# Norm gains turned by TensorE, idle products ahead of the first scores, another order of the first loads, and the second half of w_in rounded over eight pairs

## The chip, the cores and the metric

One core of a Trainium2 chip. The metric is the device time of one execution in microseconds (us), lower is better. PE is TensorE (its weight loads are PEld), DVE is VectorE, ACT is ScalarE, POOL is GpSimd, SP is the engine that issues most transfers (SPq is its queue). L405 is line 405 of the kernel in question; the changed kernel's lines stand some 6 to 8 lower in the file, so the scores are L405 before and L413 after.

## The reference

```python
# q, k, v: (8, 12, 448, 64); g_q, g_k: (64,); w_in: (768, 2048); w_out: (2048, 768)
def rmsnorm(x, g):
    return x / np.sqrt(np.mean(x * x, axis=-1, keepdims=True) + 1e-06) * g
q_n, k_n = rmsnorm(q, g_q), rmsnorm(k, g_k)
scores = q_n @ k_n.transpose(0, 1, 3, 2) / sqrt(64)
attn = softmax(scores)                      # over the last axis
x = (attn @ v).transpose(0, 2, 1, 3).reshape(3584, 768)
h = x @ w_in
out = (h / (1 + exp(-h))) @ w_out
```

Both weights arrive as 64-bit floats. The kernel builds 32-bit floats from the two words of each ("rounding").

## The kernel before

48 pairs of heads are run one after the other: six pairs make a batch. TensorE is kept full by a filler: products with w_in of batches that are already done run between the scores and the weighted sums of the pair at hand (from pair 12 on; a little from pair 7 on). Each of them is done by Strassen's scheme, seven products of blocks in place of eight, so sums of blocks of w_in and x are needed, and VectorE evicts and adds.

First, the head: loads, gains, normalisation of the first pair.

```python
    load(state, 0)                       # q, k and v of pair 0, on SP's queue
    for i, g in enumerate((g_q, g_k)):   # both gains as rows, for a check of their size
        nc.scalar.dma_start(g1[:, i, :], g.rearrange("(one d) -> one d", one=1))
    load(state, 1)
    room = Room(nc, const, w_in, z)
    while room.w_in.load():              # the first eight pieces of w_in, 512 KB each
        pass
    for t, g in ((gq2, g_q), (gk2, g_k)):        # both gains as columns, twice
        for half in range(2):
            nc.gpsimd.dma_start(t[ds(half * D, D), :], g.rearrange("(d one) -> d one", one=1))
    # ... (cut)
    nc.gpsimd.tensor_tensor(out=gains, in0=gq2, in1=gk2, op=ALU.mult)
    nc.gpsimd.tensor_scalar(out=gains, in0=gains, scalar1=float(D) ** -0.5, ...)   # cut
```

Second, the ring for w_in. A piece is loaded as raw words into a slot, `open` copies its two words on ScalarE, `round` puts them together on VectorE (L106, L109, L113) and GpSimd (L117), and then loads into every slot that is free:

```python
    def round(self):
        # ... (cut: three instructions on VectorE)
            nc.gpsimd.tensor_tensor(out=wi, in0=wi, in1=low, op=ALU.add)
        while self.load():
            pass
    # ... (cut)
    def weights_in(n, point):            # called at points 0 to 3 of pair n
        if n < 2 * NPAIR:                # pairs 0 to 11: one piece per pair
            count = point == 3
        else:                            # pairs 13 to 16: three pieces per pair
            count = 2 * NPAIR < n < 2 * NPAIR + 5 and point > 0
        for _ in range(count):
            room.w_in.round()
            room.w_in.open()
        i = n - 2 * NPAIR
        if i == 0 and point > 1:
            for step in range(2):
                sum_w_in(1, 2 * (point - 2) + step)
        if i in (1, 5, 6):
            sum_w_in({1: 0, 5: 2, 6: 3}[i], point)
```

In every second pair the softmax sums of two pairs are exchanged between partitions: four small copies, then two that wait for them. Behind them, in the same queue, come the pieces of w_in and then q and k of the pair three ahead.

```python
    for n in range(last + 2):
        load(n + 3, "qk")
        # ... scores, weights_in(n, 0), filler, weights_in(n, 1) (cut)
        divide_by_sums(n)     # n even: sums, reciprocals, then the exchange on SP's queue
        # ... (cut)
        weights_in(n, 3)      # n < 12: round a piece, load the next
        normalise(n + 3)      # ScalarE squares q and k of pair n + 3
```

Of the kernel before, what the change touches and what calls it, by code (L numbers as in the profile page):

```python
# [11 lines left out]
F32 = mybir.dt.float32  # L12
AF = mybir.ActivationFunctionType
ALU = mybir.AluOpType
AX = mybir.AxisListType
# [12 lines left out]
BANK = 512  # L28
# [19 lines left out]
class Rounder:  # L48
# [39 lines left out]
    def round(self):  # L88






        i = self.rounded
        if i == len(self.pieces):
            return
        while self.opened <= i:
            self.open()
        self.rounded += 1  # L100
        dst, src, (_, raw), low = self.pieces[i]
        if src.dtype == I64:
            nc = self.nc
            wi = dst.bitcast(I32)
            high = raw.rearrange("p (n two) -> p n two", two=2)[:, :, 1]
            nc.vector.tensor_scalar(  # L106
                out=dst, in0=dst, scalar1=HIGH_MIN, scalar2=HIGH_MAX, op0=ALU.max, op1=ALU.min
            )
            nc.vector.tensor_scalar(  # L109
                out=wi, in0=wi, scalar1=3, scalar2=0x3FFFFFF8,  # L110
                op0=ALU.logical_shift_left, op1=ALU.bitwise_and,
            )
            nc.vector.scalar_tensor_tensor(  # L113
                out=wi, in0=high, scalar=-(1 << 30), in1=wi,
                op0=ALU.bitwise_and, op1=ALU.bitwise_or,
            )
            nc.gpsimd.tensor_tensor(out=wi, in0=wi, in1=low, op=ALU.add)  # L117
        while self.load():
            pass


class Room:
# [6 lines left out]
    def __init__(self, nc, pool, w_in, z):  # L129
        P = z.P  # L130
        self.NC = z.NF // self.CHUNK
        self.size1 = z.NW * self.COLS
        self.size2 = 3 * z.NW // 2 * self.COLS // 2
        self.all = pool.tile([P, self.NC * (self.size1 + self.size2)], F32, name="W")
        self.rest = self.all[:, ds(self.NC * self.size1, self.NC * self.size2)]


        n = 2 * self.COLS
        bits = self.rest.bitcast(I32)
        pieces, before = [], {}  # L140
        for i in range(self.NC):
            for c in range(z.NW):
                number = len(pieces)
                late = i >= self.NC // 2
                raw = number % (3 if late else 8)
                low = n * (3 if late else 8) + number % 2 * self.COLS
                start = self.NC // 2 * self.size2 if late else 0
                pieces.append(
                    (
                        self.chunk(i)[:, ts(c, self.COLS)],  # L150
                        w_in[ts(c, P), ts(i, self.COLS)],
                        (
                            before.get((late, raw), 7 if late else None),
                            bits[:, ds(start + raw * n, n)],
                        ),
                        bits[:, ds(start + low, self.COLS)],
                    )
                )
                before[late, raw] = number
        self.w_in = Rounder(nc, pieces)  # L160
# [13 lines left out]
def kernel(  # L174
# [22 lines left out]
    nc = tc.nc  # L197
    z = Shapes(q, w_in)
    P, D, R, J = z.P, z.D, z.R, z.J

    const = ctx.enter_context(tc.tile_pool(name="const", bufs=1))

    n = 2 * J * D
# [5 lines left out]
    state = [dict() for _ in pairs]  # L209
# [3 lines left out]
    def load(state, n, names="qkv"):  # L213
        if n >= len(pairs):
            return
        b, hp = pairs[n]
        for name in names:

            order = "p j h d" if name == "k" else "p h j d"
            t = rings[name][n % len(rings[name])]  # L220
            t = t.rearrange(f"p ({order[2:]}) -> {order}", h=2, j=J)
            nc.sync.dma_start(
                t, sources[name][b, ts(hp, 2)].rearrange(f"h (p j) d -> {order}", j=J)
            )
            state[n][name] = t if name != "k" else t.rearrange("p j h d -> p h j d")


    load(state, 0)
    g1 = const.tile([1, 2, D], F32, name="g1")
    gq2 = const.tile([P, 1], F32, name="gq2")  # L230
    gk2 = const.tile([P, 1], F32, name="gk2")
    gains = const.tile([P, 1], F32, name="gains")
    for i, g in enumerate((g_q, g_k)):
        nc.scalar.dma_start(g1[:, i, :], g.rearrange("(one d) -> one d", one=1))
    load(state, 1)
    room = Room(nc, const, w_in, z)
    while room.w_in.load():
        pass
    minus_half = const.tile([P, 1], F32, name="minus_half")
    nc.gpsimd.memset(minus_half, -0.5)  # L240
    for t, g in ((gq2, g_q), (gk2, g_k)):
        for half in range(2):
            nc.gpsimd.dma_start(t[ds(half * D, D), :], g.rearrange("(d one) -> d one", one=1))
    ident = const.tile([P, P], F32, name="ident")
    make_identity(nc, ident)
    ones = const.tile([P, D], F32, name="ones")
# [3 lines left out]

    small = const.tile([1, 1], I32, name="small")
    most = const.tile([1, 1], F32, name="most")
    both = const.tile([1, D], F32, name="both")
    nc.vector.tensor_tensor(out=both, in0=g1[:, 0, :], in1=g1[:, 1, :], op=ALU.mult)
    nc.vector.tensor_reduce(
        out=most, in_=both, axis=AX.X, op=ALU.max, apply_absolute_value=True
    )
    nc.vector.tensor_scalar(
        out=small, in0=most, scalar1=float(SCORE_MAX / D**0.5), scalar2=None, op0=ALU.is_le
    )  # L260

    nc.gpsimd.tensor_tensor(out=gains, in0=gq2, in1=gk2, op=ALU.mult)
    nc.gpsimd.tensor_scalar(
        out=gains, in0=gains, scalar1=float(D) ** -0.5, scalar2=None, op0=ALU.mult
    )


    normal = [const.tile([R, J, 2, D], F32, name=f"qn{i}") for i in range(2)]
# [44 lines left out]
            engine.tensor_tensor(out=by_head, in0=rows["q"], in1=factor, op=ALU.mult)  # L313


def store(nc, out, z, column, o, m0):


    at = 0
    while at < o.shape[0]:  # L320
        b, c = divmod(column + at, z.S)
        j, p = divmod(c, z.R)
        n = min(z.R - p, o.shape[0] - at)
        rows = out[ds(b * z.S, z.S), ds(m0, o.shape[1])].rearrange("(p j) m -> j p m", j=z.J)
        nc.sync.dma_start(rows[j, ds(p, n)], o[ds(at, n), :])
        at += n


# [1 line left out]
def bounded(  # L330
# [41 lines left out]
    def normalise(n):  # L372
        if n <= last:
            normalise_rows(
                nc, z, state[n], normal[n % 2], squares, rms[n % 4], minus_half, nc.gpsimd
            )

    def transpose(n, name):
# [349 lines left out]
    def halves_out(t):  # L728
        w = tiles[t % 2].rearrange("p (m r t c) -> p m r t c", m=HF, r=2, t=2)
        s = s_tiles[t % 2].rearrange("p (s m c) -> p s m c", s=3, m=HF)  # L730
        a11, a12, a21, a22 = (w[:, :, i, j] for j in range(2) for i in range(2))
        left_sums(a11, a12, a21, a22, s[:, 0], s[:, 1], s[:, 2])
        lefts = {"1": a11, "2": a12, "3": s[:, 2], "4": a22, "5": s[:, 0], "6": s[:, 1], "7": a21}

        def right(name, m):
            b11, b12, b21, b22, t1, t2, t4 = chunk_out(m // 2)
            return {"1": b11, "2": b21, "3": b22, "4": t4, "5": t1, "6": t2, "7": b12}[name][
                :, m % 2
            ]

        o = [outs[(2 * t + i) % len(outs)] for i in range(2)]
        done = {(i + 1, j + 1): o[i][:, ts(j, z.HALF)] for i in range(2) for j in range(2)}
        steps = [2 * i + k for i in ORDER for k in range(2)]
        part = Seven(lambda name, m: lefts[name][:, m], right, steps, z.HALF, done)
        yield from chain(part.two(), part.five())
        for i in range(2):
            if t < NT // 2 - 1 or i == 0:
                store(nc, out, z, (2 * t + i) * P, o[i], 0)
            else:
                for j in (1, 0):  # L750
                    store(nc, out, z, (2 * t + i) * P, o[i][:, ts(j, z.HALF)], j * z.HALF)


    filler = dict(work=iter(()), due=0.0, share=0.0)
# [36 lines left out]
    products = HF * 7 * HW * S  # L791
    NPAIR = z.NPAIR

    def weights_in(n, point):

        if n < 2 * NPAIR:
            count = point == 3
        else:
            count = 2 * NPAIR < n < 2 * NPAIR + 5 and point > 0
        for _ in range(count):  # L800
            room.w_in.round()
            room.w_in.open()
        i = n - 2 * NPAIR
        if i == 0 and point > 1:
            for step in range(2):
                sum_w_in(1, 2 * (point - 2) + step)
        if i in (1, 5, 6):
            sum_w_in({1: 0, 5: 2, 6: 3}[i], point)

    transpose(0, "k")  # L810
    normalise(1)
    transpose(0, "q")
    load(2, "qk")
    for n in range(last + 2):
# [5 lines left out]
        if n > 0:  # L820
# [3 lines left out]
            unload(n - 1)  # L824
            if ends and n <= last:
                sum_x([b - 2, b - 1], 1)
        transpose(n + 1, "q")
        if n == 0:
            normalise(2)
        weights_in(n, 0)  # L830
        if ends and n <= last:
# [11 lines left out]
        divide_by_sums(n)  # L843
        if n <= last:
            scores(n, 1)
        if b == 0:
            transpose(n + 1, "k")
        if n <= last:
            weigh(n, 0)
        if b > 0:  # L850
            transpose(n + 1, "k")
        if n <= last:
# [246 lines left out]
```

## Time and profile before

| | |
|---|---|
| median | 1464.22 us (1463.85 to 1465.36, 4 runs) |
| span of the profiled run | 1461.4 us |
| TensorE without a product | 36.4 us of it |
| first scores start | 14.59 us |
| scores of pair 1 start | 26.50 us |

A page of the profile gives busy time per engine. The view by windows gives it per stretch. The timeline gives instructions in order, with the idle time of the engine before each and the event that ended it in brackets. The lines are shown in the prediction below. They are read thus: TensorE is busy 98% of the span, so a change is worth what it takes from the few stretches where TensorE has nothing to do (the first 15 us, some 15 us up to 300 us) or runs slowly.

One more table serves below: the start of the first exponential of each pair, taken from the trace, because it tells where one kernel gets ahead of another. For the kernel before: pair 1 at 29.60, pair 6 at 73.59, pair 13 at 156.64, pair 21 at 311.94 us.

### The profile page before, as it was taken

To read this page: it belongs to the slowest core of one execution; us is meant where nothing else is said; L and a number is where in the kernel's file an instruction comes from. 1 tells how busy PE (TensorE), PEld (TensorE's weight loads), DVE (VectorE), ACT (ScalarE), POOL (GpSimd) and SP (SyncE) were. 2 spreads that over 40 slices of the span, in tenths; PEclk is the share of its full clock that TensorE was granted. 3 is DMA by queue.
4 is the path that set the end of the run, shared out by engine and by line. 5 is a ranking of instruction groups with operands and counts; after the bars stand their busy time and mean duration, and the time that the engine had idled before them with its cause. 6 is when DMAs were issued, how large, how long until landed. Compare 5 with 4: busy or idle time off the path is not lost.

```text
span 1461.4 us, 13997 instructions
## 1 busy us (share of the span) xinstructions
PE 1425.0 (98%) x5024; PEld 693.9 (47%) x5024; DVE 708.7 (48%) x939; ACT 540.5 (37%) x907; POOL 402.6 (28%) x258
## 2 busy tenths in 40 slices
PE   5999999999999999999999999999999999999998
PEld 2333333444444444444444445555555555555554
DVE  4988877646644455745545687722222222222220
ACT  5876566555555455555445344300000000000000
POOL 6665454333333333332322054410000000000000
PEclk9999999999999999999999999999999999999999
DMA  6543253322232232223221157422222222222220
GB/s 211 139 127 103 71 177 97 111 73 60 76 98 70 63 94 77 70 66 97 68 60 70 61 180 241 126 94 80 79 82 82 81 80 83 80 87 83 86 62 25
DMA packets 124180, 137.67 MB, mean 94 GB/s; under 512 B 50500, under 2 KB 104772, under 8 KB 124100
## 3 DMA queue, kind: packets, MB, share of 16 engines
q1 hardware_dynamic: 123968, 136.67, 31.0%
q8 instruction: 42, 0.69, 0.2%
q14 instruction: 38, 0.31, 0.1%
q0 software_dynamic: 128, 0.00, 0.0%
q10 hardware_dynamic: 4, 0.00, 0.0%
HBM read 88.48 MB, written 41.29 MB: 89 GB/s over the span
## 4 chain that ended last, share of the span: by engine, by line
PE 85%; DVE 4%; issue 1%; DMA 1%; ACT 0%; POOL 0%; SPq 0%; DVEq 0%; ACTq 0%; POOLq 0%
PE mm L531 38%; PE sc L531 14%; PE sc L405 8%; PE av L421 8%; PE av L531 7%; PE tr L531 7%; PE tr L449 1%; PE tr L391 1%; PE tr L386 1%; DVE work L433 1%; DVE rms L303 1%; DMA rows<-in_v_dram 0%; DVE work L453 0%; DVE stage L482 0%; DVE W L482 0%
## 5 line engine op out<-in xcount | busy, mean ns | idle before, releaser
L410 ACT ACTIVATE work<-sc,rms 112x448 f32<-112x448 f32 x384 | 212.4, 638 | 185.6 <-PE sc L405 158.1
L531 PE MATMUL mm<-x,W 128*128 128x448 f32 x648 | 261.1, 542 | 3.5 <-DVE parts L482 3.2
L309 POOL TENSOR_TENSOR rms<-rms,minus_half 112x16 f32<-112x16 f32 (+1 forms) x49 | 176.3, 3598 | 265.0 <-DVE rms L305 264.4
L531 PE MATMUL mm<-sums_x,W 128*128 128x448 f32 x480 | 195.2, 542 | 3.2 <-DVE parts L482 1.6
L405 PE MATMUL sc<-work 64*112 64x448 f32 x768 | 172.5, 568 | 1.7 <-ACT work L395 0.8
L531 PEld LDWEIGHTS mm<-x,W 128*128 128x128 f32 x648 | 118.5, 190 | 110.2 <-issue 98.9
L421 PE MATMUL av<-work,rows 112*64 112x448 f32 x768 | 165.5, 552 | 0.0
L433 DVE TENSOR_TENSOR work<-work 112x896 f32<-112x896 f32 x144 | 158.0, 1098 | 1.8
L551 POOL TENSOR_TENSOR parts<-parts,stage 128x448 f32<-128x448 f32 (+1 forms) x37 | 41.8, 1129 | 327.5 <-DVE parts L482 323.1
L531 PEld LDWEIGHTS mm<-sums_x,W 128*128 128x128 f32 x480 | 87.7, 190 | 83.3 <-issue 70.6
L405 PEld LDWEIGHTS sc<-work 64*112 64x112 f32 x768 | 61.7, 174 | 103.7 <-issue 77.5
L421 PEld LDWEIGHTS av<-work,rows 112*64 112x64 f32 x768 | 46.6, 136 | 105.4 <-issue 98.0
L551 POOL TENSOR_TENSOR parts<-parts,W 128x384 f32<-128x384 f32 x9 | 9.0, 996 | 307.8 <-DVE parts L482 307.8
L453 DVE RECIPROCAL work<-tr 128x448 f32<-128x448 f32 x25 | 73.9, 2957 | 39.8 <-PE tr L449 39.7
L482 DVE TENSOR_TENSOR stage<-mm,parts 128x448 f32<-128x448 f32 (+1 forms) x59 | 36.2, 616 | 83.5 <-PE mm L531 51.9
L538 ACT COPY stage<-mm 128x448 f32<-128x448 f32 (+1 forms) x34 | 17.9, 526 | 156.4 <-PE mm L531 146.7
L662 ACT ACTIVATE stage<-stage 128x896 f32<-128x896 f32 x64 | 58.5, 945 | 36.6 <-DVE stage L482 35.7
L531 PE MATMUL mm<-W,work 128*128 128x384 f32 x204 | 68.6, 486 | 0.0
L531 PE MATMUL sc<-W,work 128*128 128x384 f32 x192 | 64.5, 486 | 0.0
L397 DVE TENSOR_SCALAR work<-tr,gains 128x448 f32<-128x448 f32 x36 | 24.6, 684 | 75.4 <-PE tr L391 75.4
L303 DVE TENSOR_REDUCE rms<-qn 112x8 f32<-112x512 f32 x49 | 33.4, 682 | 53.4 <-ACT qn L302 53.3
L313 POOL TENSOR_TENSOR qn<-rows,rms 112x512 f32<-112x512 f32 x47 | 56.6, 1205 | 3.7
(157 smaller groups left out, 1784.6 us busy)
## 6 DMA issues: line engine op xcount, KB each, us to landing
hidden<-stage SPq DMA_DIRECT2D x64, 448.0 KB, 2.9
work<-hidden SPq DMA_DIRECT2D x7, 2048.0 KB, 9.6
x<-hidden SPq DMA_DIRECT2D x7, 2048.0 KB, 8.8
W<-in_moe_w_in_dram SPq DMA_DIRECT2D x24, 512.0 KB, 5.2
rows<-in_moe_w_out_dram SPq DMA_DIRECT2D x32, 384.0 KB, 3.2
rows<-in_q_dram SPq DMA_DIRECT2D x48, 224.0 KB, 3.6
rows<-in_k_dram SPq DMA_DIRECT2D x48, 224.0 KB, 4.2
rows<-in_v_dram SPq DMA_DIRECT2D x48, 224.0 KB, 2.7
```

The costliest lines, as they stand in the source:

```text
L303: nc.vector.tensor_reduce(out=rms[:, i], in_=t, axis=AX.X, op=ALU.add)
L309: nc.gpsimd.tensor_tensor(out=flat, in0=flat, in1=half, op=ALU.pow)
L313: engine.tensor_tensor(out=by_head, in0=rows["q"], in1=factor, op=ALU.mult)
L405: nc.tensor.matmul(banks[:, h, 0:S], kT[rows, ts(j, R)], qT[n % 2][rows, :], start=True, stop=True,)
L410: nc.scalar.activation(e[j][:, h, :], banks[:, h, 0:S], AF.Exp, scale=rms[n % 4][:, 1, h, j : j + 1])
L421: nc.tensor.matmul(st["av"][ds(h * D, D), :], st["v"][:, h, j, :], e[j][:, h, :], start=(j == 0), stop=(j == J - 1),)
L433: nc.vector.tensor_tensor(out=t, in0=e[0] if j == 1 else t, in1=e[j], op=ALU.add)
L453: nc.vector.reciprocal(out=r[0], in_=t)
L482: nc.vector.tensor_tensor(out=out, in0=a, in1=b, op=ALU.add)
L531: nc.tensor.matmul(t, self.left(name, s), self.right(name, s), start=s == ends[0], stop=s == ends[1])
L551: nc.gpsimd.tensor_tensor(out=u2, in0=u2, in1=p5, op=ALU.add)
L662: nc.scalar.activation(t, t, AF.Silu)
```

## The change

Its intent: start the scores earlier, at TensorE's full clock, and take VectorE's load in pairs 13 to 16 apart.

```diff
@@ Rounder.round
-        while self.load():
-            pass
+        for _ in range(2):
+            self.load()
@@ Room: nine early slots, two late ones; the low words stay in the slot
-                raw = number % (3 if late else 8)
-                low = n * (3 if late else 8) + number % 2 * self.COLS
-                start = self.NC // 2 * self.size2 if late else 0
+                raw = number % (2 if late else 9)
+                start = (self.NC - 1) * self.size2 if late else 0
+                words = bits[:, ds(start + raw * n, n)]
 ...
-                        bits[:, ds(start + low, self.COLS)],
+                        words.rearrange("p (n two) -> p n two", two=2)[:, :, 0],
@@ the head
-    load(state, 0)
+    load(state, 0, "qk")
+    load(state, 1, "qk")
 ...
-    load(state, 1)
     room = Room(nc, const, w_in, z)
-    while room.w_in.load():
-        pass
+    for n in range(2):
+        room.w_in.load()
+        load(state, n, "v")
 ...
-    for t, g in ((gq2, g_q), (gk2, g_k)):
-        for half in range(2):
-            nc.gpsimd.dma_start(t[ds(half * D, D), :], g.rearrange("(d one) -> d one", one=1))
 ...
-    nc.gpsimd.tensor_tensor(out=gains, in0=gq2, in1=gk2, op=ALU.mult)
+        keep_busy(4)          # idle products of the identity with itself
+        nc.tensor.transpose(column, both.rearrange("p two d -> p (two d)"), ident[0:1, 0:1])
+        nc.vector.tensor_scalar_mul(out=gains, in0=column, scalar1=float(D) ** -0.5)
+        keep_busy(12)
@@ the dates of rounding and sums, i = n - 12
+    rounds = {(1, 1), (1, 3), (3, 1), (3, 3), (4, 1), (4, 3), (5, 3)}
+    rounds |= {(6, 1), (6, 3), (7, 1), (7, 3), (8, 0)}
+    sums_at = {(0, 2): (1, (0, 1)), (0, 3): (1, (2, 3))}
+    for chunk, at in ((0, (2, 0)), (2, (5, 0)), (3, (8, 1))):
+        for step in range(4):
+            sums_at[at[0] + (at[1] + step) // 4, (at[1] + step) % 4] = chunk, (step,)
@@ the order of the first pairs
-    transpose(0, "k")
     normalise(1)
+    transpose(0, "k")
     transpose(0, "q")
 ... pair 0: the transposes of pair 1 come behind all scores and the first weighted sums of pair 0;
 ... pair 1's q is normalised by VectorE, not GpSimd; the last stores alternate between two queues
```

More of the change, by code (lines that the diff above doesn't have):

```diff
@@ L152, in __init__ @@
                         (
-                            before.get((late, raw), 7 if late else None),
-                            bits[:, ds(start + raw * n, n)],
+                            before.get((late, raw), 8 if late else None),
+                            words,
                         ),
-                        bits[:, ds(start + low, self.COLS)],
+                        words.rearrange("p (n two) -> p n two", two=2)[:, :, 0],
                     )
@@ L225, in load @@
             state[n][name] = t if name != "k" else t.rearrange("p j h d -> p h j d")
-    load(state, 0)
+    load(state, 0, "qk")
+    load(state, 1, "qk")
     g1 = const.tile([1, 2, D], F32, name="g1")
-    gq2 = const.tile([P, 1], F32, name="gq2")
-    gk2 = const.tile([P, 1], F32, name="gk2")
     gains = const.tile([P, 1], F32, name="gains")
@@ L252 @@
     most = const.tile([1, 1], F32, name="most")
-    both = const.tile([1, D], F32, name="both")
-    nc.vector.tensor_tensor(out=both, in0=g1[:, 0, :], in1=g1[:, 1, :], op=ALU.mult)
+    both = const.tile([1, 2, D], F32, name="both")
+    wide = [g1[:, i : i + 1, :].to_broadcast([1, 2, D]) for i in range(2)]
+    nc.vector.tensor_tensor(out=both, in0=wide[0], in1=wide[1], op=ALU.mult)
     nc.vector.tensor_reduce(
-        out=most, in_=both, axis=AX.X, op=ALU.max, apply_absolute_value=True
+        out=most, in_=both[:, 0, :], axis=AX.X, op=ALU.max, apply_absolute_value=True
     )
@@ L260, with keep_busy @@
     )
-    nc.gpsimd.tensor_tensor(out=gains, in0=gq2, in1=gk2, op=ALU.mult)
-    nc.gpsimd.tensor_scalar(
-        out=gains, in0=gains, scalar1=float(D) ** -0.5, scalar2=None, op0=ALU.mult
-    )
+    with tc.tile_pool(name="ps_first", bufs=1, space=bass.MemoryType.PSUM) as ps_first:
+        idle = ps_first.tile([P, P], F32, name="idle")
+        column = ps_first.tile([P, BANK], F32, name="column")[:, 0:1]
+        def keep_busy(n):
+            for _ in range(n):
+                nc.tensor.matmul(idle, ident, ident, start=True, stop=True)
+        keep_busy(4)
+        nc.tensor.transpose(column, both.rearrange("p two d -> p (two d)"), ident[0:1, 0:1])
+        nc.vector.tensor_scalar_mul(out=gains, in0=column, scalar1=float(D) ** -0.5)
+        keep_busy(12)
     normal = [const.tile([R, J, 2, D], F32, name=f"qn{i}") for i in range(2)]
@@ L313, in normalise_rows, with store @@
             engine.tensor_tensor(out=by_head, in0=rows["q"], in1=factor, op=ALU.mult)
-def store(nc, out, z, column, o, m0):
-    at = 0
+def store(nc, out, z, column, o, m0, *queues):
+    at, queues = 0, queues or [nc.sync]
     while at < o.shape[0]:
@@ L324, in store @@
         rows = out[ds(b * z.S, z.S), ds(m0, o.shape[1])].rearrange("(p j) m -> j p m", j=z.J)
-        nc.sync.dma_start(rows[j, ds(p, n)], o[ds(at, n), :])
+        queues[0].dma_start(rows[j, ds(p, n)], o[ds(at, n), :])
+        queues = queues[1:] + queues[:1]
         at += n
@@ L374, in normalise @@
             normalise_rows(
-                nc, z, state[n], normal[n % 2], squares, rms[n % 4], minus_half, nc.gpsimd
+                nc, z, state[n], normal[n % 2], squares, rms[n % 4], minus_half,
+                nc.gpsimd if n > 1 else nc.vector,
             )
@@ L750, in halves_out @@
                 for j in (1, 0):
-                    store(nc, out, z, (2 * t + i) * P, o[i][:, ts(j, z.HALF)], j * z.HALF)
+                    store(
+                        nc, out, z, (2 * t + i) * P, o[i][:, ts(j, z.HALF)], j * z.HALF,
+                        nc.scalar, nc.sync,
+                    )
     filler = dict(work=iter(()), due=0.0, share=0.0)
@@ L792, in bounded @@
     NPAIR = z.NPAIR
-    def weights_in(n, point):
-        if n < 2 * NPAIR:
-            count = point == 3
-        else:
-            count = 2 * NPAIR < n < 2 * NPAIR + 5 and point > 0
-        for _ in range(count):
+    rounds = {(1, 1), (1, 3), (3, 1), (3, 3), (4, 1), (4, 3), (5, 3)}
[4 more added lines that the diff above has]
+            sums_at[at[0] + (at[1] + step) // 4, (at[1] + step) % 4] = chunk, (step,)
+    def weights_in(n, point):
+        i = n - 2 * NPAIR
+        if (i < 0 and point == 3) or (i, point) in rounds:
             room.w_in.round()
             room.w_in.open()
-        i = n - 2 * NPAIR
-        if i == 0 and point > 1:
-            for step in range(2):
-                sum_w_in(1, 2 * (point - 2) + step)
-        if i in (1, 5, 6):
-            sum_w_in({1: 0, 5: 2, 6: 3}[i], point)
+        chunk, steps = sums_at.get((i, point), (0, ()))
+        for step in steps:
+            sum_w_in(chunk, step)
+    normalise(1)
     transpose(0, "k")
-    normalise(1)
     transpose(0, "q")
@@ L826, in bounded @@
                 sum_x([b - 2, b - 1], 1)
-        transpose(n + 1, "q")
-        if n == 0:
+        if n > 0:
+            transpose(n + 1, "q")
+        else:
             normalise(2)
@@ L845, in bounded @@
             scores(n, 1)
-        if b == 0:
+        if b == 0 and n > 0:
             transpose(n + 1, "k")
@@ L849, in bounded @@
             weigh(n, 0)
+        if n == 0:
+            transpose(n + 1, "q")
+            transpose(n + 1, "k")
         if b > 0:
```

## The prediction

> **What bounds the kernel now.** I read the page's first section first, then busy time per window, then the timeline of the first 30 us, then the windows again cut at each pair of heads, then the waits.
>
> The page (busy us, share of the span, instructions):
>
> ```profile
> PE 1425.0 (98%) x5024; PEld 693.9 (47%) x5024; DVE 708.7 (48%) x939; ACT 540.5 (37%) x907; POOL 402.6 (28%) x258
> ```
>
> TensorE is the bound: 1425.0 of 1461.4 us, so only 36.4 us of the span are without a product. Whatever this change does, it must find its time in those 36.4 us, or in products that run slower than they could. The windows say where they lie (columns: window, length, then busy us and instruction count of PE, PEld, DVE, ACT, POOL, then clock, DMA share, GB/s):
>
> ```profile
> 0.00:6.30 6.30, 0.00 (x0) 0.02 (x1) 1.31 (x5) 2.22 (x4) 3.24 (x12) 1.00 0.47 127
> 6.30:14.60 8.30, 2.00 (x10) 1.31 (x10) 2.63 (x5) 2.73 (x5) 3.64 (x4) 1.00 1.01 334
> 14.60:20.20 5.60, 4.26 (x13) 1.73 (x13) 0.37 (x2) 2.32 (x4) 3.97 (x2) 1.00 1.04 384
> ...
> 300.00:400.00 100.00, 99.92 (x386) 42.61 (x385) 59.89 (x75) 52.10 (x85) 31.46 (x17) 1.00 0.26 74
> ...
> 850.00:1400.00 550.00, 548.76 (x1659) 314.85 (x1658) 174.15 (x249) 57.74 (x107) 70.47 (x67) 1.00 0.33 103
> ...
> 1450.00:1462.00 12.00, 5.35 (x17) 2.85 (x15) 1.11 (x2) 0.00 (x0) 0.00 (x0) 0.82 0.25 72
> ```
>
> From 300 us to the last store TensorE never waits. The idle time is 12.6 us ahead of the first scores (6.3 + 8.30 - 2.00), about 1.9 us from there to 30 us, some 15 us between 30 and 300 us (of which 9.2 in the stretch that the change rearranges, below), and 6.1 us after the last product. DMA is at 1.0 from 6.3 to 20.2 us.
>
> The timeline of the head (start, duration, engine, line, operation; in brackets the idle time before and its releaser):
>
> ```profile
> 8.54 0.19 POOL L262 TENSOR_TENSOR gains<-gq,gk 128x1 f32<-128x1 f32 x1 [4.31 <-DMA gk<-in_g_k_dram]
> 8.68 3.27 POOL L309 TENSOR_TENSOR rms<-rms,minus_half 112x8 f32<-112x8 f32 x2
> 11.95 0.23 POOL L263 TENSOR_SCALAR gains<-gains 128x1 f32<-128x1 f32 x1
> 12.27 0.64 ACT L395 ACTIVATE work<-tr,gains 128x448 f32<-128x448 f32 x1 [5.44 <-POOL gains L263]
> 14.59 3.33 PE L405 MATMUL sc<-work 64*112 64x448 f32 x8 [0.62 <-ACT work L387]
> ...
> 22.04 0.63 ACT L302 ACTIVATE qn<-rows 112x512 f32<-112x512 f32 x1 [1.21 <-DMA rows<-in_q_dram]
> ...
> 26.50 1.76 PE L405 MATMUL sc<-work 64*112 64x448 f32 x8 [0.46 <-ACT work L395]
> ```
>
> The first scores (14.59) wait for a chain that begins with a tiny load: gains on GpSimd waits for g_k until 8.54, the powers of the norms queue behind it, the second gains instruction behind those, and ScalarE's copy of k behind that. Eight score records took 3.33 us at 14.59 and 1.76 us at 26.50: the first run at half speed.
>
> **What the Trainium skill says.**
> 1. "TensorE: Matmul & The Clock Gate", Part 1 (the HAM clock gate): the array starts at half rate and is released after one fully busy window of about 3.4 us. The trace agrees: records of this shape take 536 ns at best and 1086 at worst. The clock column reads 1.00 in both stretches, so it must be read from durations.
> 2. "DMA: Bandwidth & Descriptors", Specifications: first byte about 1 us on GpSimd's path, about 0.6 us on the sync and scalar path. The trace is harsher: the 0.2 KB loads from GpSimd's queue took 3.7 to 4.9 us to land; the same vectors as rows from ScalarE's queue, issued until 1.48, were used at 3.06.
> 3. "GPSIMD Engine Reference", Key points: GpSimd shares its SBUF interfaces with VectorE and they contend. The trace agrees: VectorE's first rounding step (L106) takes 0.42 us alone and 1.24 us at 193.91, beside GpSimd.
> 4. Same page, "Performance pitfalls for Q7 kernels": a read costs more when its byte step exceeds 8. Low words in place are read with a step of exactly 8, so by the page without penalty; no run shows it yet (L117 takes 1274 ns on packed words).
>
> **The change part by part.**
>
> *a. Gains by TensorE, fewer early bytes, another start order: the head.* Removed: four DMA issues on GpSimd (2.3 us of its sequencer, 1.28 to 3.6) and the wait to 8.54. Then, step by step, with durations of the same instructions:
> - The row sums of q are scaled by 4.92 in the old trace. The power of q can start there: half of 3.27, so 1.63 us, to 6.6. k lands at 6.2 as before (its load is still the second), squares, sum and scale to 7.75, VectorE's q product (0.69) to 8.4, power of k to 9.4.
> - 4 + 12 idle products. A 128-row product of 448 columns takes 4.53/6 = 0.755 us warm (12 records in the merged rows, less the overhang), so 128 columns 0.216 us warm and 0.43 cold. They start near 1.7 us (identity without the DMA issues before it). Cold throughout they end near 8.6; if released halfway, near 7.7. The gains column is turned near 3.5 us; gains is ready by 8.7 on VectorE, in its turn.
> - The branch, k's transposes (0.6 warm) near 8.5 to 9.2. ScalarE now squares both of pair 1's inputs first: k of pair 1 landed at 9.6, with v of pair 0 no longer ahead (224 KB) about 8.3; squared to 9.0. Copy of k to about 9.8, q's transposes, copy of q: first scores at about 11.0 instead of 14.6, saving 3.6 us.
> - Warm scores and transposes: 1.57 us for each of two score groups. In the order after, all scores of pair 0 stand before pair 1's transposes, so no GpSimd product (18.16 to 19.2) stands between. Exponentials of the first half 11.9 to 14.3 (4 x 0.58), squares of pair 2 1.3 us, second half to 17.9, copy of q 0.6, transposes of k 0.6, copy of k 0.65: scores of pair 1 at about 19.8 instead of 26.50. Saving at this point: **6.7 us**, which contains the 3.6 and the warm clock.
> From there the order is that of before and ScalarE (10.00 of 10 us busy from 30 to 40) sets the pace, so the saving is only shifted, not enlarged.
>
> *b. Second half of w_in over eight pairs: the middle.* Windows cut at the first scores of pairs 13, 14, 15, 16, 17, 18:
>
> ```profile
> 155.53:176.20 20.67, 18.86 (x70) 7.94 (x70) 16.66 (x24) 9.49 (x18) 10.00 (x6) 1.00 0.20 62
> 176.20:195.43 19.23, 18.71 (x76) 7.79 (x75) 17.30 (x24) 14.33 (x23) 11.38 (x7) 1.00 0.53 161
> 195.43:216.52 21.09, 18.36 (x68) 7.47 (x67) 16.87 (x24) 12.25 (x21) 11.24 (x7) 1.00 0.60 180
> 216.52:236.40 19.88, 18.78 (x75) 7.80 (x74) 16.16 (x21) 14.56 (x23) 10.74 (x7) 1.00 0.44 122
> 236.40:255.35 18.95, 18.11 (x68) 7.55 (x67) 12.44 (x17) 10.64 (x17) 8.16 (x5) 1.00 0.26 80
> 255.35:274.57 19.22, 18.72 (x76) 7.79 (x75) 13.18 (x15) 10.27 (x18) 5.91 (x4) 1.00 0.34 102
> ```
>
> TensorE loses 1.8, 0.5, 2.7, 1.1, 0.8, 0.5 = 7.5 us here (pair 12 ahead loses 1.7 more, which the change doesn't touch), waiting for evictions on VectorE. VectorE's w_in work isn't reduced, it is moved: a rounding is 0.42 + 0.43 + 0.69 = 1.54 us, a sum step 0.95 us. Before: three roundings in each of pairs 13 to 16, with four sums in 13 also, four sums in 17 and 18. After: two roundings in 13, 15, 16, 18, 19, four sums in 14, four sums and a rounding in 17, a rounding and three sums in 20. Pairs with three roundings alone lost (0.5 + 2.7 + 1.1)/3 = 1.45; I take 0.5 for two. Pairs with four sums lost 0.67. So after: 5 x 0.5 + 3 x 0.67 + 0.3 = 4.8. Saving **2.7 us**.
>
> *c. Last stores on two queues.* The last four issues span 4.89 us on one queue, most of it waiting for VectorE's last sum (1455.54 + 0.56). One issue of about 0.5 us comes off the end: **0.3 us**.
>
> *d. Low words in place*: nothing, if point 4 holds.
>
> Sum: 6.7 + 2.7 + 0.3 = 9.7 us; 1464.06 - 9.7 = **1454.4 us**.
>
> **The rivals.**
> - *The new wait takes the old one's place.* ScalarE must square k of pair 1 before the first copy, and TensorE must finish 16 idle products before the first transpose. If k lands at 9.6 as before and the products stay cold, scores start near 12.2, and with a cold relapse in the gap between pair 0 and pair 1 the head gives 3 us. For: ScalarE is in order; against: eight 512 KB loads no longer queue at 5.27. Total then 1459.
> - *VectorE's load decides the middle, not its bunching.* The work is the same, and pairs 19 and 20, which lose nothing today, get a share. For: pairs 17 and 18 lose though they round nothing. Then b gives 0: 1457. The other way, short bursts vanish behind 18 us of products per pair: b gives 7: 1450.
> - *The early weights become late.* Two pieces instead of eight are loaded up front, so a rounding or an input load behind two 512 KB pieces could wait. For: inputs are used about one pair (9 us) after their issue; against: 3.6 to 5.2 us to landing, and DMA share 0.3 to 0.6 there. It would cost up to 3 us.
>
> **Range and chances.** Head 3 to 9, middle 0 to 6, stores 0 to 0.6: not all ends at once, so 1449 to 1459. Two per cent is 29.3 us; the whole idle time of 36.4 us, less the 6.2 until k lands and some 5 after the last sum, is 25, plus about 4.5 of cold clock. Faster by over 2% is all but impossible: 0.01. Slower by 2% would need a stall of 29 us in a static order with loads far from full: 0.01. Same: 0.98.
>
> **What would show it.** In the changed trace: gains on VectorE before 9 us and no wait of GpSimd for g_k; the first scores near 11 us with eight records in 1.76 us; pair 1's scores near 20 us; every later start earlier by 6 to 7 us until pair 12; VectorE near 14 us per pair in 13 to 20 and TensorE's idle time there near 5 us; rounding on GpSimd still near 1274 ns. Wrong would be: scores past 12 us behind ScalarE's squares or idle products, score records still at 1086 ns, a wait for rows of q or k after 25 us, or the idle time of pairs 13 to 20 at 7 us again.

## The result

The changed kernel takes 1458.38 us (median of 4 runs, 1456.55 to 1459.26) against 1464.22 us. The ratio is 0.9957 (95% interval 0.9940 to 0.9974). A ratio is the mean time of one kernel's fast runs over that of the other's fast runs of the same rounds, so not quite the ratio of the medians quoted. The profiled run is the slowest of the four, 1459.26 us, with a span of 1457.2 us; that of the kernel before took 1463.25 us, so the two profiles lie 4.0 us apart and the medians 5.8.

The page of the changed kernel, busy time:

```profile
PE 1429.4 (98%) x5057; PEld 699.0 (48%) x5057; DVE 708.3 (49%) x941; ACT 540.4 (37%) x907; POOL 397.9 (27%) x251
```

27.8 us are left without a product, but 5.9 us of the products (2.08 + 3.81) are idle ones that compute nothing.

The windows of the changed kernel (columns as in the prediction):

```profile
6.30:14.60 8.30, 5.86 (x37) 3.18 (x35) 3.68 (x9) 5.09 (x11) 5.46 (x3) 1.00 0.89 240
...
20.20:24.30 4.10, 4.10 (x17) 1.16 (x13) 3.83 (x7) 4.10 (x9) 2.39 (x3) 0.68 0.44 118
...
50.00:75.00 25.00, 21.49 (x94) 7.51 (x94) 19.87 (x26) 19.56 (x37) 14.65 (x7) 0.86 0.63 171
```

The head is fuller, as meant. New is the last line: 3.5 us idle between 50 and 75 us, where the kernel before lost 1.0, and the clock column falls to 0.86.

The timeline of the changed kernel's head:

```profile
5.19 1.65 POOL L315 TENSOR_TENSOR rms<-rms,minus_half 112x8 f32<-112x8 f32 x1 [3.81 <-DVE rms L311]
...
7.75 0.15 DVE L270 TENSOR_SCALAR gains<-column 128x1 f32<-128x1 f32 x1
...
8.80 0.63 ACT L403 ACTIVATE work<-tr,gains 128x448 f32<-128x448 f32 x1 [0.46 <-PE tr L399]
...
10.72 1.76 PE L413 MATMUL sc<-work 64*112 64x448 f32 x8 [0.62 <-ACT work L395]
...
19.30 3.29 PE L413 MATMUL sc<-work 64*112 64x448 f32 x8 [0.79 <-ACT work L403]
```

GpSimd's powers start at 5.19 instead of 8.68 us, the gains are there at 7.9, k is copied at 8.80 instead of 12.27, and the first scores run at full clock from 10.72 us. Pair 1's scores start at 19.30 instead of 26.50 us. But they take 3.29 us: the clock has fallen back.

The first exponential of each pair, in the changed kernel less that of before (from the two traces; negative is earlier):

```
pair    1      3      4      5      6      9     12     13     14     16     17     19     20     21     47
     -7.20  -6.69  -4.63  -2.60  -1.88  -2.10  -1.80  -1.80  -3.87  -9.51  -7.03  -6.78  -5.75  -4.08  -4.09
```

This difference is called the shift below, and this row is the whole account of these two profiles. The head brings 7.2 us. **4.8 us are lost between pairs 3 and 6.** The middle brings 7.7 us up to pair 16 and gives 5.4 of them back by pair 21, 2.3 net. From pair 21 on the two kernels run at the same pace to a hundredth.

The stall, in the changed kernel's timeline of 42 to 63 us (lines of SP's queue, ScalarE and TensorE):

```profile
42.48 1.05 SPq L68 DMA_DIRECT2D W<-in_moe_w_in_dram  x2
...
43.58 0.43 SPq L222 DMA_DIRECT2D rows<-in_q_dram  x1
44.05 0.65 SPq L222 DMA_DIRECT2D rows<-in_k_dram  x1
...
48.90 0.63 ACT L308 ACTIVATE qn<-rows 112x512 f32<-112x512 f32 x1 [1.30 <-DMA rows<-in_q_dram]
...
50.67 0.63 ACT L308 ACTIVATE work<-rows 112x512 f32<-112x512 f32 x1 [1.15 <-DMA rows<-in_k_dram]
...
54.40 1.71 PE L457 MATMUL mm<-work,ones 112*32 112x448 f32 x6 [3.05 <-DVE work L441]
56.05 3.33 PE L413 MATMUL sc<-work 64*112 64x448 f32 x8
```

And the same place in TensorE's timeline of the kernel before:

```profile
59.04 0.95 PE L449 MATMUL mm<-work,ones 112*32 112x448 f32 x6 [0.99 <-DVE work L433]
59.92 1.76 PE L405 MATMUL sc<-work 64*112 64x448 f32 x8
```

Read it as a chain. SP's queue is held by the exchange of the sums until 42.4 us, then issues two pieces of w_in, then q and k of pair 6. ScalarE gets them 5.3 and 6.6 us after their issue (43.58 to 48.90, 44.05 to 50.67), although it wants to square q at 47.6. In ScalarE's program the exponentials of pair 4 stand behind the squares; VectorE's sums stand behind the exponentials; TensorE stands behind the sums, 3.05 us instead of 0.99. After that TensorE runs at half clock for a while: six records in 1.71 us instead of 0.95, eight scores in 3.33 instead of 1.76.

The middle, windows of the changed kernel cut at the scores of pairs 14, 16, 17 and 20 (to the next pair's):

```profile
172.32:190.77 18.45, 18.45 (x75) 7.87 (x74) 14.93 (x19) 11.40 (x17) 7.38 (x4) 1.00 0.47 138
...
208.91:228.26 19.35, 18.51 (x75) 7.87 (x74) 16.07 (x20) 12.06 (x19) 10.91 (x7) 1.00 0.48 136
228.26:248.31 20.05, 18.09 (x67) 7.55 (x66) 13.30 (x19) 11.75 (x19) 7.79 (x5) 1.00 0.35 102
...
285.34:306.80 21.46, 18.79 (x76) 7.79 (x75) 17.76 (x21) 8.82 (x17) 9.42 (x6) 1.00 0.12 31
```

Pairs 13 to 15 now lose nothing (pair 14 with its four sums: 18.45 of 18.45). Pairs 16, 17 and 20 lose 0.8, 2.0 and 2.7. In pair 20 VectorE's sum step waits for GpSimd's part of the rounding just before it, and then runs slowly beside GpSimd. Two sums of GpSimd fill 294.60 to 296.83 us, and VectorE's step, which takes 0.95 us elsewhere, ends 0.81 us after them:

```profile
294.68 2.96 DVE L490 TENSOR_TENSOR W<-W 128x768 f32<-128x768 f32 x1 [1.70 <-POOL W L117]
...
300.56 0.60 PE L399 MATMUL tr<-ident,rows 112*128 112x112 f32 x4 [1.76 <-DVE work L461]
```

### The profile page after: what moved, and what is told of

Its sections match the earlier page's. It is cut to its first block, busy times and chain, and to the rows that moved or that the text cites. A ratio compares the mean times of both kernels' runs of the same rounds, so it can differ in the third digit from the quotient of the medians.

```text
span 1457.2 us, 14067 instructions
## 1 busy us (share of the span) xinstructions
PE 1429.4 (98%) x5057; PEld 699.0 (48%) x5057; DVE 708.3 (49%) x941; ACT 540.4 (37%) x907; POOL 397.9 (27%) x251
## 4 chain that ended last, share of the span: by engine, by line
PE 84%; DVE 3%; DMA 1%; issue 1%; ACT 1%; POOL 0%; SPq 0%; ACTq 0%; DVEq 0%; POOLq 0%
PE mm L539 38%; PE sc L539 13%; PE sc L413 8%; PE av L429 8%; PE av L539 7%; PE tr L539 7%; PE tr L457 1%; PE tr L399 1%; PE tr L394 1%; DVE work L461 1%; DVE work L441 1%; DMA hidden<-stage 0%; DMA W<-in_moe_w_in_dram 0%; DVE rms L309 0%; DVE W L490 0%
```

## The experiments

Theories after the first look. **A**: the lost 4.8 us come from what stands ahead of q and k in SP's queue, above all the second piece of w_in. **Rivals**: the bytes in flight at that time, wherever they stand; the exchange; or a part of the head's gain that was never there. And for the gains: they work only together with the loads, or each for itself. Every kernel gave the correct result. Each ran 5 rounds, against 9 runs of the kernel before on the same chip (medians 1463.74, 1463.87 and 1463.54 us in the three batches).

### One piece instead of two

```diff
@@ changed kernel, Rounder.round
-        for _ in range(2):
-            self.load()
+        self.load()
```

> The changed kernel with one piece of w_in loaded after each rounding instead of two. Theory A (in pair 4 two 512 KB pieces stand in the queue ahead of q and k of pair 6, ScalarE waits 1.30 and 1.15 us for them, TensorE stops for 3.05 us and falls to half clock): the stall of 4.8 us between 46.5 and 62 us goes, pair 5's scores start near 57 instead of 61.9 us, total near 1453.6. Rival (the wait comes from the exchange of sums ahead in the same queue, not from the pieces): pair 5 still at 61 us or later, total near 1458.4.

Measured: 1455.17 us (1452.85 to 1456.76), ratio 0.9943 (0.9930 to 0.9957). The shift is -6.61 at pair 3, -5.48 at pair 5, -5.01 at pair 6, -8.69 at pair 21 and later. So 1.6 us are lost around pair 4 and not 4.8. ScalarE's and TensorE's timelines of this run:

```profile
49.83 0.63 ACT L307 ACTIVATE work<-rows 112x512 f32<-112x512 f32 x1 [1.00 <-DMA rows<-in_k_dram]
```

```profile
53.56 0.95 PE L456 MATMUL mm<-work,ones 112*32 112x448 f32 x6 [2.12 <-DVE work L440]
```

q no longer waits, k waits 1.00 us, and after an idle time of 2.12 us the six records still take 0.95 us: the clock held. What follows: the second piece made most of the stall. Halving the pieces halves bytes and position alike, so this run doesn't tell the two apart.

### Two pieces, behind q and k

```diff
@@ changed kernel, Rounder.round and the loop over pairs
-        for _ in range(2):
-            self.load()
+        for _ in range(2):
+            if self.loaded >= self.behind:      # 12 for w_in, 0 for w_out
+                self.load()
...
         load(n + 3, "qk")
+        for _ in range(2 if n > 0 else 0):
+            if room.w_in.loaded < room.w_in.behind:
+                room.w_in.load()
```

> The changed kernel with the same two pieces of w_in per pair in the first pairs, but issued behind q and k of the pair instead of ahead. Theory A (what stands ahead of q and k in the queue decides): ScalarE's waits of 1.30 and 1.15 us for q and k of pair 6 go, as with one piece, TensorE's wait before pair 4's sums falls from 3.05 to 2.1 us or less, total near 1455. Rival (the bytes moved in that stretch decide, wherever they stand): as the changed kernel, near 1458.4.

Measured: 1452.86 us (1452.29 to 1456.87), ratio 0.9925 (0.9912 to 0.9939). The profiled run is the slowest of the five: its shift is only -4.12 at pair 3 (pair 1's scores took 3.33 us at half clock, and q of pair 2 was waited for 0.91 us), but it stays: -4.55 at pair 6, -4.31 at pair 9. The place of the stall in TensorE's timeline:

```profile
54.49 0.95 PE L459 MATMUL mm<-work,ones 112*32 112x448 f32 x6 [0.55 <-DVE work L443]
```

0.55 us instead of 3.05, with two pieces per pair still: theory A holds. That position decides and not bytes is shown less clearly, for the new place also spreads the pieces. In the changed kernel four were issued within 5 us around q and k of pair 6 (from 42.48 and 45.46 us), here two from 46.40 and two from 51.02 us. Landing does follow the bytes ahead: q of pair 6 landed 2.84 us after its issue at 45.09 us, with no piece in flight, and q of pair 7, issued at 49.92 us behind two pieces, took 6.80 us. But that one wasn't wanted before 60.2 us. The Trainium skill says of the rings in "DMA: Bandwidth & Descriptors", section "Queues, rings and completion order": on each engine the descriptors are consumed in ring order. The traces agree: q of pair 6 came to ScalarE 5.3 us after its issue behind two pieces, and isn't waited for when it is ahead of them. This version loses 2.0 us between pairs 9 and 10 (ScalarE waits 1.63 us for q of the pair three ahead), where the first pieces of the second half are still issued ahead of q.

### The exchange behind q and k

```diff
@@ changed kernel: the six copies are kept in a list and issued one pair later
-            for i in range(2): ...          # in divide_by_sums(n)
+            owed_exchange.append(own)
...
         load(n + 3, "qk")
+        exchange()                          # the six copies owed
```

> The changed kernel with the exchange of the sums (six small copies whose last two wait for the first four) issued behind the next pair's q and k instead of ahead. Theory: q and k of pair 6 are then issued near 39 us instead of 43.6 us and land before ScalarE asks; the stall of pair 4 goes altogether, with the 1.1 us that is left when only one piece is loaded: total near 1453. Rival (only the pieces matter): near 1458.4.

Measured: 1461.2 us (1459.46 to 1463.3), ratio 0.9982 (0.9968 to 0.9995). At the place in question the expectation held: q was issued at 36.94 us, and the shift is -6.45 at pair 3, -6.75 at pair 6, -6.61 at pair 9, nothing lost. So the head's gain was there to be kept. The total did not follow, for it lost 7 us between pairs 9 and 11. TensorE's timeline there:

```profile
114.73 1.17 PE L457 MATMUL tr<-work,ones 112*32 112x448 f32 x2 [3.15 <-ACT work L395]
```

There two pieces wait in SP's queue 10.11 us for a free slot, the late exchange stands behind them, VectorE's division waits for it, and the sums behind the division. The run shows that the exchange had its part in the stall, and that moving it by a whole pair makes another.

### One piece, behind q and k

```diff
@@ as two pieces behind, but
+        for _ in range(1 if n > 0 else 0):
```

> Both cures at once: one piece of w_in per pair in the first pairs, issued behind q and k. Theory A (what stands ahead of q and k decides): the shift of pair 3 (6.6 us where the clock holds) is kept through pair 9, total near 1452, at or below the run with two pieces behind. Rival (one piece was already enough and the order adds nothing): 1455 as with one piece ahead.

Measured: 1464.21 us (1461.63 to 1465.53), ratio 1.0005 (0.9991 to 1.0019). A miss, far from 1452. The shift falls from -6.41 at pair 3 to +0.58 at pair 6. ScalarE's timeline says why:

```profile
50.83 0.66 ACT L83 ACTIVATE W<-W 128x512 int32<-128x512 uint32 x1 [4.06 <-DMA W<-in_moe_w_in_dram]
```

It isn't q that is late now but the piece itself. With one piece per pair the stock of loaded pieces doesn't grow: the piece loaded at the top of a pair is opened at its end, and where the exchange holds the queue it lands too late (issued at 44.12, landed at 50.80 us). Both cures together take the margin that each leaves alone.

### Idle products also behind pair 1's transposes

```diff
@@ as the run just told, in pair 0
             transpose(n + 1, "q")
+            keep_busy(3)
             transpose(n + 1, "k")
+            keep_busy(3)
```

> As the run with one piece behind, with three idle products after pair 1's transposes of q and three after those of k, to fill TensorE's gaps near 18 to 19 us. Theory (in about half of the profiles the clock relapses at 19 us, and pair 1's scores then take 3.3 us, which explains a part of the spread of the changed kernel): pair 1's scores always at 1.76 us, median 0.5 to 1 us lower and less spread than the run without them. Rival ([...]relapse anyway, or the products delay k): no difference.

Measured: 1465.34 us (1463.16 to 1466.69), ratio 1.0014 (1.0000 to 1.0028), against 1464.21 without them in the same batch. In the profile the gaps of 0.62 and 0.79 us are filled and pair 1's scores run at full clock, as meant. But there is no gain in time, the base was a bad one, and the full clock isn't shown to come from the new products: in three profiles without them (one piece, the middle undone, the last rounding moved) it held too. What goes with it is the end of the 16 idle products of the head. Where they ended at 7.70 to 7.98 us (four profiles, one of them with a gap of 2.04 us before pair 1 as well) pair 1's scores took 2.96 to 3.33 us; where they ran longer at half clock and ended at 8.34 to 9.58 us, as here (four profiles), 1.76 us. The later end also costs: first scores at 12.30 us here and at 11.00 in the base. (The profile with all early loads is left out: it had a gap of 9.7 us before pair 1.) Inconclusive on the worth of it.

### The head without its idle products

```diff
@@ changed kernel
-        keep_busy(4)
         nc.tensor.transpose(column, ...)
         nc.vector.tensor_scalar_mul(out=gains, ...)
-        keep_busy(12)
```

> The changed kernel without its 16 idle products. Theory: the first scores start at the same 10.7 us (they wait for ScalarE's copy of q), but at half clock: 3.3 us instead of 1.8 for eight records in each group of pair 0, about 1.5 to 2.5 us later at pair 1's scores (19.3 us now), total near 1460.4. Rival (ScalarE's exponentials set the pace of pair 0 anyway): nothing lost, 1458.4. Rival (the products hold the start up): the scores start earlier, 1457.

Measured: 1459.64 us (1458.5 to 1460.59), ratio 0.9972 (0.9958 to 0.9985), against the changed kernel's 0.9957. By the ratios the products are worth 0.0015 of 1464 us, 2.2 us; the intervals overlap. In the profile pair 0's exponentials start 1.8 us later than in the changed kernel (13.67 and 11.83) and pair 1's 2.2 us later (24.59 and 22.41). Pair 1's scores start at 21.49 instead of 19.30 us, and take 3.19 us, at half clock, as in the changed kernel. The first theory held near its total (1460.4) and its delay of pair 1, but not in "the same 10.7 us": the first scores start at 11.73 us, for the transposes ahead of them run at half clock too (0.98 and 1.01 us instead of 0.58 and 0.60).

### The gains alone

```diff
@@ kernel before: gains as a row turned by TensorE; nothing else, no idle products
-    for t, g in ((gq2, g_q), (gk2, g_k)): ...   # four loads on GpSimd's queue
+        nc.tensor.transpose(column, both.rearrange("p two d -> p (two d)"), ident[0:1, 0:1])
+        nc.vector.tensor_scalar_mul(out=gains, in0=column, scalar1=float(D) ** -0.5)
```

> The kernel before with the gains as a row turned by TensorE, and nothing else. Theory (the gains' wait is off the path by itself, since inputs of pair 2 still stand behind 4 MB of w_in and land at 22 us): first scores near 11 us, but pair 1's first exponential still near 29 us, total within 1.5 us of the kernel before. Rival (the gains' wait carries the head): pair 1's exponentials near 25 us and total near 1459.5.

Measured: 1463.82 us (1461.7 to 1466.26), ratio 1.0002 (0.9989 to 1.0016). Pair 0 is ahead by 3.18 us, pair 1 by 1.28, pair 5 and all later ones by 0.6 to 0.8. ScalarE's line:

```profile
20.70 0.63 ACT L300 ACTIVATE qn<-rows 112x512 f32<-112x512 f32 x1 [3.14 <-DMA rows<-in_q_dram]
```

q of pair 2 lands at 20.7 us behind eight pieces, and the second half of pair 0's exponentials stands behind its squares. A new wait takes the place of the old one, as expected.

### The loads alone

```diff
@@ kernel before, only the loads
-    load(state, 0)
+    load(state, 0, "qk")
+    load(state, 1, "qk")
-    load(state, 1)
-    while room.w_in.load():
-        pass
+    for n in range(2):
+        room.w_in.load()
+        load(state, n, "v")
 ... and two loads after each rounding instead of all that fit
```

> The kernel before with only the new order and number of loads (q and k of two pairs first, two pieces, two more after each rounding). Theory: first scores at 14 us still (the gains wait), pair 1's first exponential near 26 us instead of 29.6 because q of pair 2 no longer lands at 22 us, and the stall at pair 4 takes it back: total within 1.5 us of the kernel before. Rival (the loads carry the head): pair 1 near 23 us, total near 1460.

Measured: 1465.37 us (1464.56 to 1468.99), ratio 1.0018 (1.0004 to 1.0031). First scores at 14.75 us, pair 1's first exponential at 28.40 (1.20 ahead, not 3.6), and from pair 3 to pair 6 the shift goes from -1.19 to +2.00. So the stall comes with the loads by themselves: 3.2 us of it here. The total missed the forecast of 1.5 us by little: 1.8 us behind the kernel before by the medians, slower if anything.

### The changed head, with the old bulk of loads

```diff
@@ changed kernel
     for n in range(2):
-        room.w_in.load()
         load(state, n, "v")
+    while room.w_in.load():
+        pass
```

> The changed kernel with all nine early pieces loaded at the start, behind both v, as the kernel before had eight. Theory (the head's gain needs both, the gains early and the queue short): first scores still near 11 us, but q of pair 2 lands behind 4 MB near 21 us, so pair 1's first exponential is near 28 us instead of 22.4; no two pieces per pair then, so no stall at pair 4: total near 1459. Rival (the gains and idle products carry the head alone): pair 1 near 23 us, total near 1453.

Measured: 1462.97 us (1461.52 to 1465.06), ratio 0.9998 (0.9985 to 1.0012). Pair 0 is 4.41 us ahead and pair 1 is 2.55 us *behind* the kernel before. ScalarE's line:

```profile
22.81 0.63 ACT L309 ACTIVATE qn<-rows 112x512 f32<-112x512 f32 x1 [8.54 <-DMA rows<-in_q_dram]
```

8.54 us of waiting for q of pair 2, and in the changed order pair 1's transposes stand behind all of pair 0, so TensorE has a gap of 9.7 us. I had expected 28 us for pair 1 and 1459 in total; it was 32.15 and 1462.97. No stall followed at pair 4: +3.37 at pair 3, +3.53 at pair 6.

### The middle undone, and the middle alone

```diff
@@ changed kernel with the ring and the dates of before ("undone");
@@ kernel before with the ring and the dates of after ("alone")
-                raw = number % (2 if late else 9)
+                raw = number % (3 if late else 8)
 ... and weights_in as before; the other way round in the second run
```

> The changed kernel with the old ring for w_in and the old dates for rounding and sums (three pieces per pair in pairs 13 to 16). Theory: the new dates gain 6.3 us over pairs 13 to 16 and give back about 4.0 in pairs 17 to 20, so undoing costs 2.3 us: total near 1460.7. Rival (VectorE's total decides, dates give nothing): 1458.4. Rival (all of the middle's gain is kept): 1464.

> The kernel before with only the new ring, low words in place and the new dates for rounding and sums; its head and its order of loads are untouched. Theory: the same 2.3 us net as in the run that undoes them, total near 1461.9, with the first scores at 14.6 us as before. If the two runs disagree by over 2 us, head and middle aren't independent.

Measured, undone: 1459.45 us (1458.28 to 1462.63), ratio 0.9978 (0.9965 to 0.9992). The shift stays at -3.80 from pair 13 to -3.91 at pair 21: without the new dates there is neither the gain of 7.7 nor the loss of 5.4. Alone: 1462.7 us (1462.21 to 1463.12), ratio 0.9995 (0.9981 to 1.0008): +1.59 at pair 13 (nine pieces instead of eight are loaded ahead of the start, the likely cause), and -1.11 at pair 21, so the dates bring 2.7 us. Over the nine profiles with exactly the new dates the gain from pair 13 to pair 21 is 1.9 (exchange behind) to 3.2 us (one piece, two pieces behind, all early), with 2.3 in the changed kernel and 2.7 alone. The times alone would not have settled it; the shifts do.

### The last rounding away from the last sums

```diff
@@ changed kernel, dates
-    rounds |= {(6, 1), (6, 3), (7, 1), (7, 3), (8, 0)}
+    rounds |= {(6, 1), (6, 3), (7, 1), (7, 2), (7, 3)}
 ... and the last chunk's sums at (8, 0), (8, 2), (8, 3), (9, 0) instead of (8, 1) to (9, 0)
```

> The changed kernel with the last piece rounded in pair 19 (point 2) instead of pair 20, and the sums of the last chunk no longer at the point behind that rounding. Theory: the shift against the kernel before stays at its value of pair 19 and doesn't fall by the 1.7 us of pairs 20 and 21 (VectorE waits 1.70 us for GpSimd's part of the rounding and then takes 2.96 us for a step of 0.95): total near 1456.6. Rival (three roundings in one pair cost as much): 1458.4.

Measured: 1459.18 us (1456.48 to 1460.35), ratio 0.9962 (0.9948 to 0.9976), no different from 0.9957. The shift still falls, from -4.90 at pair 19 to -2.95 at pair 21, 1.95 us against 2.70 in the changed kernel. The long wait for VectorE's reciprocals is gone, but one of 0.81 us for an eviction is new in pair 19, and one of 0.91 us in pair 20 stays as it was. The rival was nearer: the work is moved, and it costs about as much where it lands.

## Why the prediction was right or wrong

The time lies in the range (1449 to 1459) but at its upper end: 9.7 us of saving were forecast, 5.8 came.

- **The head: right.** Gains before 9 us (7.9), k of pair 1 squared before the first copy (from 7.74), idle products ended at 7.7 us (forecast 7.7 or 8.6), first scores at 10.72 (forecast 11.0), pair 1's scores at 19.30 (forecast 19.8), shift 6.6 to 7.2 us (forecast 6.7). Its reason had a gap: the gains were put first, the loads second. The runs show that neither is worth more than 1.3 us at pair 1 alone, and both together with the new order 7.2, of which 2.2 are the idle products by the profiles; no run has the order alone. The full clock at pair 1 was forecast and isn't certain: it held in four of the eight profiles compared above, those in which the idle products ended late, and relapsed in that of the changed kernel. So a part of the agreement is luck: in these eight profiles the first scores start anywhere from 10.66 to 12.30 us.
- **"From there the order is that of before ... so the saving is only shifted": wrong.** This is the step that failed. The stall between pairs 3 and 6 took 4.8 us out of 6.7. It was named as a rival, "the early weights become late", and left out of the sum with "up to 3 us". The argument against it used the time from issue to landing (3.6 to 5.2 us) and a use one pair after the issue. In the trace q was issued 4.8 us into the pair, because exchange and pieces stood ahead, and was wanted 4.0 us after its issue. The relapse of the clock after the idle time of 3.05 us was not in the working at all.
- **The middle: right in size, partly in mechanism.** 2.7 us forecast, 2.3 in the changed kernel and up to 3.2 in other runs. Idle time of pairs 13 to 20 was forecast at 4.8 us; the windows give 6.3 (before, over the same pairs, 7.5). So only 1.2 of the 2.3 us are idle time saved; the rest is product time, 0.27 us less in each of pairs 13 to 16 with the same number of records, which was not in the working. The idle time wasn't spread evenly: 0.0 in pairs 13 to 15, 5.5 in pairs 16, 17 and 20. The term that was mis-sized is the 0.67 us for four sums: pairs 14, 17 and 20 were to lose 2.3 us and lost 4.6. The five pairs with two roundings were to lose 2.5 and lost 1.6.
- **The stores: not seen in the time.** From the last product to the end the spans leave 6.18 us in the changed kernel and 6.09 before. Over all profiles it is 5.6 on average with two queues (10 profiles, 5.3 to 6.2) and 6.1 with one (4 profiles, 5.6 to 6.5). 0.3 us was forecast; 0.5 fits, and the scatter is larger.
- **Low words in place: right.** GpSimd's rounding takes 1290 ns in the median, with 1274 before.

What stays open: why pairs 16 and 17 lose 2.8 us. In the trace TensorE waits 0.84 us at 222.45 us for VectorE's reciprocals, which start only after a rounding (217.26 to 219.45 us), and 1.80 us at 237.03 us for an eviction on VectorE. VectorE had waited 5.13 us for ScalarE's squares, and these stand behind a copy for which ScalarE waited 5.18 us, for a store, until 229.75 us. No run took one of these waits alone away. And how much of the run-to-run scatter of the changed kernel (2.7 us, before 1.5) is the clock's relapse.

Of the versions tried, the two pieces behind q and k have the lowest median, 1452.86 us, 0.9925 of the kernel before; the interval overlaps that of one piece. Each version was profiled once, and times of the changed kernel scatter by 2.7 us, so shifts that differ by a few tenths between profiles aren't told apart.

## What to carry to other kernels

A load that was moved out of the start must go somewhere: find, in the one queue that issues it, which transfer it now stands ahead of, and compare that transfer's deadline with its new time of issue, not with its time to landing alone. Two waits in series at the head, here gains and inputs, have to be removed together, and each looks worthless by itself. When two kernels share a tail, lay the starts of the same step side by side: it shows to a hundredth where time was won and where it was given back, when the total shows only the difference.

## What the Trainium skill lacked or had wrong

- "TensorE: Matmul & The Clock Gate", Part 1, lets the clock fall back after an idle window of about 3.4 us, and tells of a kernel in which short waits between groups were enough, without giving their size. Here it relapsed at 19.3 us with no gap over 0.8 us in the 6 us before (0.04, 0.62 and 0.79 us): eight score records took 3.29 us instead of 1.76. Of the gaps from 2.0 to 3.2 us in the profiles, six were followed by half-clock records (2.04, 2.25, 2.44, 2.62, 3.05 and 3.15 us) and three weren't (2.12, 2.41 and 2.56).
- The same Part warns that clock events in a trace can be unreliable. This form of it is on no page: the clock column shows 1.00 from 14.6 to 24.3 us in the kernel before, where score records take up to 1086 ns instead of 536, and 0.68 and 0.86 at the later relapses of the changed kernel. Durations are the safer sign.
- "DMA: Bandwidth & Descriptors", Anatomy of one DMA, fits 2.0 us plus the bytes to a transfer on GpSimd's path. Loads of 0.2 KB from GpSimd's queue took 3.7 to 5.3 us to land while the first bulk loads were in flight (the prediction's 4.9 is a median of two, and it compared landing with the page's time to the first byte, which isn't the same). No run shows the reason.
